# Retention attention and a low-rank channel mixer on one core: when the second weight matrix is loaded, and where the third batch's attention stands

## The chip, the cores and the metric

The program runs on one core of one Trainium2 chip. A core has five engines with instruction queues of their own: TensorE (PE) for matrix products, VectorE (DVE), ScalarE (ACT), GpSimd (POOL), and SyncE (SP), which here only issues transfers. Sixteen DMA engines move data between HBM and the on-chip memory. The time is the device time of one execution in microseconds (us); of several executions the median is given. The span of a profile is the stretch from the first to the last instruction of one profiled execution.

## The reference

Attention without a softmax, with a decay per head, and behind it a mixer over positions of rank 32 and a two-layer channel network:

```python
B, H, S, D = 8, 8, 576, 64
scores = q @ k^T / sqrt(D)
gamma  = 1 - 2.0 ** (-5.0 - arange(H))
ret    = scores * where(i >= j, gamma ** (i - j), 0)
x      = (ret @ v) laid out as (B, S, H * D)          # 8 x 576 x 512
u      = x + (x^T @ U @ V)^T                          # U 576 x 32, V 32 x 576
out    = u + max(u @ w_ch1, 0) @ w_ch2                # w_ch1 512 x 2048, w_ch2 2048 x 512
```

All inputs and the output are float32. The kernel multiplies in bfloat16 and adds up in float32.

## The kernel before

**Tiling.** Batches are taken in pairs. A pair has 1152 positions, which are nine chunks of 128; chunk 4 holds the last 64 positions of the even batch and the first 64 of the odd one. A chunk is named (pair, index), so (1,3) is the fourth chunk of the second pair. Attention is done chunk by chunk with a running state for each head: `SC` makes the scores inside a chunk, `ST` what the chunk adds to the state, `RV` the product of the masked scores with v, `QS` the product of q with the state, `XS` scales the sum into x. The sum of `RV` of one chunk, `SC` of the next, and so on is a "section".

**Getting a chunk ready.** `load` (L225) issues three transfers on SP's queue (six for chunk 4) that bring k, q and v as float32 into 15 staging buffers. `prep` (L562) casts k on DVE (L250) and q on ACT (L252), scales v on POOL (L261), and issues a transposing transfer `qkT<-qk` on SP's queue (L269). `SC` and `QS` read the transposed tile.

**The channel network.** `Y1` (L492) makes one block of 128 hidden features for the positions of a batch: four matrix products into one of three PSUM buffers (`ps_big`), for an odd batch twice, with 4 and with 1 chunk of positions or with 3 and 2; ACT then applies Relu (L505) into `y1`. `Y2` (L529) adds up 16 products over the hidden features for one chunk of positions, four to an item; DVE adds u (L523), and POOL issues the store (L526). w_ch2 comes in eight pieces of two feature blocks each, which `load_w2(f)` (L207) issues on POOL's queue.

**Order.** The program order is written by hand, and every engine and every queue works in that order. `startup` and `first_stretch` (L914) do the first pair's attention and the even batch's first layer. Then the loop at L1047 makes one stage for each b from 1 to 7. In a stage `merge` (L22) runs through the `main` items, which are matrix products of the channel network with a cost in ns each, and puts in between two queues of other items, each with a place between 0 and 1: an item is emitted ahead of the first main item at which the cost done so far has reached its place times the sum of costs. The first queue, `fill`, holds the next batch's attention sections, the casts of the state (on ACT, between the sections), and the mixer (`MA`, `MH`, and `MT`, which from the second pair on is a transposing transfer `uT<-u` on SP's queue). `spread` (L16) gives these items even places from 0 to 0.82. The second queue holds the loads and the preps of later chunks, with the places of the table `places` (L1038).

Stage b=1 has the remaining ten `Y1` blocks of the first odd batch (f=6 to 15; the first six are in `first_stretch`), then `Y2` of both batches of the first pair. Its main items cost 10.8 + 13.8 + 17.3 = 41.9 us. Stages 2, 4 and 6 have 27.6 us of main items, stages 3, 5 and 7 have 34.6 us. Stage 1 holds the attention of the third batch (chunks (1,0) to (1,4)), stage 2 that of the fourth, and so on.

**Weights before.** `first_stretch` issues `load_w2` for 0 and 2 after the last unit of attention, and those for 4 to 14 in a row behind `prep(NI + 1)` (L1017).

Of the kernel before, what the change touches and what calls it, by code (L numbers as in the profile page):

```python
# [10 lines left out]
BF16 = mybir.dt.bfloat16  # L11
# [4 lines left out]
def spread(fill, lead=0.82):  # L16

    n = len(fill)
    return [((k + 0.5) / n * lead, fn) for k, fn in enumerate(fill)]


def merge(main, *queues):  # L22

    total = sum(c for c, _ in main)
    queues = [sorted(q, key=lambda x: x[0]) for q in queues]
    done = 0.0
    for cost, fn in main:
        for q in queues:
            while q and q[0][0] * total <= done:
                q.pop(0)[1]()  # L30
        fn()
        done += cost
    for q in queues:
        for _, fn in q:
            fn()
# [7 lines left out]
def kernel(  # L43
# [11 lines left out]
    nc = tc.nc  # L55
# [5 lines left out]
    P = 128  # L61
    HALF = 64
    NHP = H // 2
    NF = dff // P
# [9 lines left out]
    def pool(name, bufs, **kw):  # L74
        return ctx.enter_context(tc.tile_pool(name=name, bufs=bufs, **kw))

    consts = pool("consts", 1)
# [18 lines left out]

    ident = consts.tile([P, P], BF16, name="ident")
    tri = consts.tile([P, P], BF16, name="tri")
    s_f = consts.tile([P, 2, NHP * D], FP32, name="s_f")
    retz = []  # L100
    triU = consts.tile([P, 2, P], BF16, name="triU")
# [74 lines left out]
    def make_uo():  # L176
        ps = ps_s.tile([P, 5, R], FP32, tag="pss", name="pu_o")
        nc.tensor.matmul(ps, swap, U_E, start=True, stop=True)
        nc.scalar.activation(out=U_O[0:HALF, 1:5, :], in_=ps[0:HALF, 0:4, :], func=AF.Copy)
        nc.scalar.activation(out=U_O[HALF:P, :, :], in_=ps[HALF:P, :, :], func=AF.Copy)  # L180
# [26 lines left out]
    def load_w2(f):  # L207
        nc.gpsimd.dma_start(
            out=w2_sb[:, f:f + 2, :],
            in_=moe_w_ch2[f * P:(f + 2) * P, :].rearrange("(f p) d -> p f d", p=P),  # L210
        )
# [61 lines left out]
    st = {}  # L273
# [454 lines left out]
    def T_J(r, pool_=None, tag="big"):  # L728
        c = ch[0, J]
        pst = (pool_ or ps_big).tile([P, 2 * NHP, P], BF16, tag=tag, name="pst")  # L730
        for j in range(2):
            for hp in range(NHP):
                nc.tensor.transpose(
                    pst[:, j * NHP + hp, r], c["qk"][r, j, hp * P:(hp + 1) * P],
                    ident[r, r])
        if "qkT" not in c:
            c["qkT"] = qkT_pool.tile([P, 2 * NHP, P], BF16, tag="qkT", name="qkT")
        nc.scalar.activation(out=c["qkT"][:, :, r], in_=pst[:, :, r], func=AF.Copy)
# [67 lines left out]
    def startup():  # L806
# [99 lines left out]
        for cc in range(NCC):  # L906
# [4 lines left out]
            else:  # L911
                nc.vector.tensor_copy(out=o, in_=i_)

    def first_stretch():  # L914

        ys = iter([fn for _, fn in y1_items(0)])

        def y(n):
            for _ in range(n):
                fn = next(ys, None)  # L920
                if fn is not None:
                    fn()

        _, MH0, _, outs0 = mixer_items(0, 0, split=True)
        MA1, MH1, MT1, outs1 = mixer_items(0, 1, split=True)
        T_J(HI, ps_s, "pss")
        y(1)
        make_uo()
        SC_J(HI)
        mask_J(HI)  # L930
        y(1)
        acc = pss_tile()
        ST_J(HI, acc)
        Sblk(acc, 0)
        y(1)

        def unit(u, slots, last):
            cast_unit(u)
            load_w1(u)
            scale_u(u, 0, nc.gpsimd)  # L940
            scale_u(u, 1, nc.gpsimd)
            if not last:
                y(1)
            T_u(u, 1, nc.vector)
            T_u(u, 0, nc.scalar)
            y(2)
            SC_u(u, 0, ps_sc, "psc")
            mask_u(u, 0)
            y(1)
            ST_u(u, LO, acc, False)  # L950
            Sblk(acc, slots[1])
            SC_u(u, 1, ps_sc, "psc")
            mask_u(u, 1)
            y(1)
            if not last:
                ST_u(u, HI, acc, False)
                Sblk(acc, slots[2])
            else:
                prep(NI)
                load(*order[NI + 2], (1, 0, 2))  # L960
            RV_u(u, 0)
            QS_u(u, 0, slots[0])
            QS_u(u, 1, slots[1])
            if last:
                RV_J(HI)
                XS_J(HI)
                y(1)
            RV_u(u, 1)
            XS_u(u)

        load(*order[NI], (1, 0, 2))
        load(*order[NI + 1], (1, 0, 2))
        unit(2, (0, 1, 2), False)
        unit(3, (2, 3), True)
        load_w2(0)
        load_w2(2)
        for n in range(2):
            retz.append(ret_pool.tile([P, H, P], BF16, tag="ret", name="ret"))
            nc.gpsimd.memset(retz[n], 0.0)
        xT = [None] * NCC  # L980

        def to_xT(ccs, chunks):
            for cc in ccs:
                if xT[cc] is None:
                    pool_, tag = (ps_sc, "psc") if cc < 2 else (ps_o, "po")
                    t = pool_.tile([P, 2, dm], FP32, tag=tag, name="xT")
                    xT[cc], xT[cc + 1] = t[:, 0, :], t[:, 1, :]
                for i in chunks:
                    nc.tensor.matmul(
                        xT[cc][:, (i - J - 1) * P:(i - J) * P],  # L990
                        st["x", 0][:, i, cc * P:(cc + 1) * P], ident,
                        start=(i == J + 1), stop=True, skip_group_check=True,
                    )

        to_xT((0, 1), (5, 6))
        y(1)
        to_xT((0, 1), (7, 8))
        MA1()
        to_xT((2, 3), (5, 6, 7, 8))
        y(1)  # L1000
        for cc in range(NCC):
            g = slice(cc * R, (cc + 1) * R)
            nc.tensor.matmul(
                xT[cc], st["a", 1][g, :], V4[g, 2 * HALF:2 * HALF + 4 * P],
                start=False, stop=True, skip_group_check=True,
            )
        for cc in range(NCC):
            copy((nc.scalar, nc.vector)[cc // 2], st["uT", 1][:, 1:5, cc, :],
                 xT[cc].rearrange("p (s t) -> p s t", t=P))
        y(16)  # L1010
        Y1, rest = y1_items(1, by_seg=True)
        Y1(0, 0)
        MH1((J,))
        Y1(1, 0)
        prep(NI + 1)
        load(*order[NI + 3], (1, 0, 2))
        for f in range(4, NF, 2):  # L1017
            load_w2(f)
        Y1(2, 0)
        MT1((J,))  # L1020
        MH0(outs0[0])
        for f in range(3, 6):
            Y1(f, 0)
        MH1((5, 6, 7, 8))
        for f in range(6):
            Y1(f, 1)
        return rest[6:]

    with tc.manual_schedule():
        early_consts()  # L1030
        startup()
        y1_left = first_stretch()

        def placed(loads, preps):
            return ([(p, lambda g=g: load(*order[g], (1, 0, 2))) for g, p in loads]
                    + [(p, lambda g=g: prep(g)) for g, p in preps])

        places = {  # L1038
# [6 lines left out]
        }  # L1045
        gl, gp = NI + 4, NI + 2
        for b in range(1, B):  # L1047
            pr, par = divmod(b, 2)
            fill, lead = [], 0.82
            if b + 1 < B:  # L1050
                fill = attn_items((b + 1) // 2, (b + 1) % 2) + mixer_items(
                    (b + 1) // 2, (b + 1) % 2)
            main = y1_items(par) + y2_items(pr, par)
            if b == 1:
                main = y1_left + y2_items(0, 0) + y2_items(0, 1)
                fill = [idle] + fill
            at_l, at_p = places.get(b, ((), ()))
            aux = placed(list(zip(range(gl, gl + len(at_l)), at_l)),
                         list(zip(range(gp, gp + len(at_p)), at_p)))
            gl, gp = gl + len(at_l), gp + len(at_p)  # L1060
            merge(main, spread(fill), aux)
        assert gl == len(order) and gp == len(order)

# [28 lines left out]
```

## Time and profile before

| what | us |
|---|---|
| median of 3 runs | 326.59 (325.59 to 331.24) |
| the profiled execution's own time | 329.42 |
| its span | 327.5 |
| PE busy within the span | 315.9 (96%) |
| DVE busy | 157.3 (48%) |
| ACT busy | 135.5 (41%) |
| POOL busy | 80.2 (24%) |

The granted TensorE clock was 0.999 of full over the span. The page gives the busy time of each engine, the busy share in forty slices, the chain that ended last, and the costliest groups of instructions. Idle time of an engine other than PE costs something only where PE then waits for it. The rows used are shown where the argument uses them; a timeline row has start, duration, engine, line, operation, tile, the number of instructions that were merged, and in brackets the idle time before it with what ended it.

### The profile page before, as it was taken

Reading aid. Unit: us, or ns where it says so; the run is one execution under the profiler, and the core shown is the slowest. Engines: PE = TensorE matmul, PEld = TensorE weight load, DVE = VectorE, ACT = ScalarE, POOL = GpSimd, SP = SyncE. Lnnn points to the kernel's source line nnn. Section 1 sums busy time; section 2 is a strip of 40 time slices with the busy share of each in tenths; the row PEclk is TensorE's granted clock in tenths of the full one; section 3 lists DMA queues with packets and bytes.
Section 4 is the critical chain, followed back from the end, with each engine's and each line's share of the span. In section 5 each row is a group of like instructions: output and inputs, shape, how many; then the busy total and the mean of one; then the engine's idle time right before and its main releaser. Section 6 shows DMA issues by size and latency. Waiting matters only on the chain.

```text
span 327.5 us, 8608 instructions
## 1 busy us (share of the span) xinstructions
PE 315.9 (96%) x3704; PEld 174.4 (53%) x3704; DVE 157.3 (48%) x266; ACT 135.5 (41%) x292; POOL 80.2 (24%) x114
## 2 busy tenths in 40 slices
PE   7799999998899999999999999999999999999996
PEld 3465554654444455457744455457754455467544
DVE  5383554465544456545754357544754465510022
ACT  2557656753110275038720275038720363047400
POOL 5586548012321310122111221122211300110000
PEclk9999999999999999999999999999999999999999
DMA  7999999999996998399992999399993930430012
GB/s 204 233 208 271 228 202 168 197 165 150 253 224 161 256 192 152 90 235 191 178 205 58 246 231 174 90 248 178 204 178 80 211 67 3 115 96 2 0 71 92
DMA packets 151318, 53.27 MB, mean 163 GB/s; under 512 B 131984, under 2 KB 148752, under 8 KB 151280
## 3 DMA queue, kind: packets, MB, share of 16 engines
q1 hardware_dynamic: 144512, 40.40, 69.9%
q0 software_dynamic: 6768, 12.32, 15.9%
q8 instruction: 29, 0.48, 0.6%
q14 instruction: 9, 0.07, 0.1%
HBM read 36.85 MB, written 9.44 MB: 141 GB/s over the span
## 4 chain that ended last, share of the span: by engine, by line
PE 79%; DMA 12%; SPq 5%; POOL 1%; DVE 1%; issue 1%; ACT 0%; DVEq 0%
PE ps_y L534 35%; PE ps_y L500 34%; DMA qkT<-qk 5%; DMA stage_t<-in_q_dram 3%; DMA w_sb<-in_moe_w_ch_dram 3%; SPq L582 2%; PE psc L285 2%; DMA stage_t<-in_v_dram 2%; PE po L340 1%; PE ph L441 1%; PE ps_y L545 1%; PE psc L296 1%; PE po L353 1%; SPq L235 1%; SPq L269 1%; PE pa L414 1%
## 5 line engine op out<-in xcount | busy, mean ns | idle before, releaser
L505 ACT ACTIVATE y<-ps_y 128x384 bf16<-128x384 f32 (+2 forms) x192 | 89.5, 490 | 110.5 <-PE ps_y L500 109.4
L500 PE MATMUL ps_y<-uT,w_sb 128*128 128x512 bf16 (+3 forms) x768 | 132.8, 326 | 1.0 <-DMA w_sb<-in_moe_w_ch_dram 0.5
L534 PE MATMUL ps_y<-w_sb,y 128*128 128x512 bf16 x560 | 126.2, 379 | 0.0
L500 PEld LDWEIGHTS <-w_sb 128*128 128x128 bf16 x768 | 69.8, 98 | 49.9 <-issue 1.3
L534 PEld LDWEIGHTS <-y 128*128 128x128 bf16 x560 | 52.7, 98 | 61.5
L523 DVE TENSOR_TENSOR o_sb<-ps_y,u 128x512 f32<-128x512 f32 (+2 forms) x38 | 25.2, 663 | 76.3 <-PE ps_y L534 74.1
L261 POOL TENSOR_TENSOR vt<-stage_t,vscale 128x512 bf16<-128x512 f32 (+1 forms) x29 | 30.7, 1062 | 77.7 <-DMA stage_t<-in_v_dram 66.0
L526 POOL DMA_DIRECT2D out_dram<-o_sb x31 | 17.2, 554 | 119.4 <-DVE o_sb L523 113.6
L306 DVE TENSOR_TENSOR ret<-psc,tri 64x512 bf16<-64x512 f32 x54 | 36.9, 684 | 0.4
L322 DVE TENSOR_TENSOR s_f<-psc,s_f 128x256 f32<-128x256 f32 x42 | 17.8, 425 | 35.2 <-PE psc L296 33.0
L447 DVE TENSOR_TENSOR u<-ph,xt 128x1024 bf16<-128x1024 f32 (+3 forms) x24 | 21.8, 951 | 11.4 <-PE ph L441 11.4
L252 ACT ACTIVATE qk<-stage_t 128x512 bf16<-128x512 f32 x27 | 16.9, 626 | 16.4 <-DMA stage_t<-in_q_dram 16.4
L364 DVE TENSOR_TENSOR xt<-po,qscale 128x512 bf16<-128x512 f32 x27 | 18.7, 692 | 7.4 <-PE po L353 6.7
L331 ACT ACTIVATE s_sb<-s_f 128x512 bf16<-128x512 f32 (+1 forms) x27 | 15.5, 575 | 1.3 <-DVE s_f L320 1.3
L651 DVE TENSOR_TENSOR ret<-psc,triU 128x1024 bf16<-128x1024 f32 x8 | 9.7, 1223 | 11.4 <-PE psc L643 11.4
L420 ACT ACTIVATE a_sb<-pa 128x128 bf16<-128x128 f32 x8 | 2.2, 278 | 29.4 <-PE pa L414 29.4
L250 DVE CAST qk<-stage_t 128x512 bf16<-128x512 f32 x27 | 12.8, 479 | 0.1
L340 PEld LDWEIGHTS <-ret 128*128 128x128 bf16 x216 | 9.9, 98 | 4.4
L285 PE MATMUL psc<-qkT 64*64 64x64 bf16 x432 | 8.6, 198 | 3.7 <-DMA qkT<-qk 3.7
L600 POOL CAST qk<-stage_t 128x512 bf16<-128x512 f32 x16 | 9.7, 611 | 8.7 <-DMA stage_t<-in_q_dram 6.7
L196 PE MATMUL pw<-ident 128*128 128x512 bf16 x33 | 10.4, 456 | 1.4 <-POOL ident masks.py:199 1.4
L340 PE MATMUL po<-vt,ret 128*128 128x64 bf16 x216 | 10.7, 193 | 0.0
(112 smaller groups left out, 164.8 us busy)
## 6 DMA issues: line engine op xcount, KB each, us to landing
stage_t<-in_k_dram SPq DMA_DIRECT2D x32, 256.0 KB, 5.1
stage_t<-in_q_dram SPq DMA_DIRECT2D x32, 256.0 KB, 5.4
stage_t<-in_v_dram SPq DMA_DIRECT2D x32, 256.0 KB, 5.9
out_dram<-o_sb POOLq DMA_DIRECT2D x31, 256.0 KB, 4.0
w_sb<-in_moe_w_ch_dram POOLq DMA_DIRECT2D x4, 512.0 KB, 8.8
w_sb<-in_moe_w_ch_dram POOLq DMA_DIRECT2D x8, 256.0 KB, 9.9
stage_t<-in_k_dram SPq DMA_DIRECT2D x8, 128.0 KB, 4.9
stage_t<-in_q_dram SPq DMA_DIRECT2D x8, 128.0 KB, 5.0
```

Of the source, the lines that this page charges most:

```text
L252: nc.scalar.activation(out=t[rows, 0, :], in_=c["f", 0][rows].rearrange("p h d -> p (h d)"), func=AF.Copy)
L261: (eng or nc.gpsimd).tensor_tensor(out=c["v"][rows], in0=c["f", 2][rows], in1=vscale[rows, i, :, None].to_broadcast([n, H, D]), op=ALU.mult,)
L306: nc.vector.tensor_tensor(out=ret.rearrange("p (hp hl) i -> p hl hp i", hl=2)[t, :, :, t], in0=c["psc"][t, :, 0:SW].rearrange("p hl (hp i) ...
L322: nc.vector.tensor_tensor(out=f[:, t, :], in0=inc, in1=f[:, 1 - t, :], op=ALU.add)
L340: nc.tensor.matmul(c["po"][:, hl, hp * D:(hp + 1) * D], c["ret"][:, h, :], c["v"][:, h, :], start=(hp == 0), stop=True, skip_group_check=True,
L364: nc.vector.tensor_tensor(out=xt[:, i, :].rearrange("p (hp hl d) -> p hl hp d", hl=2, d=D), in0=c["po"][:, :, 0:NHP * D].rearrange("p hl ( ...
L447: nc.vector.tensor_tensor(out=st["u", par][:, i0 - base:i0 - base + n, w].rearrange("p s (c d) -> p c s d", c=2), in0=ph[k][:, :, 0:n, :], ...
L500: nc.tensor.matmul(ps[:, 0:n, :], w1_sb[:, cc, f * P:(f + 1) * P], st["uT", par][:, c0:c0 + n, cc, :], start=(cc == 0), stop=(cc == NCC - 1),)
L505: nc.scalar.activation(out=st["y1", par][:, f, c0 * P:(c0 + n) * P], in_=ps[:, 0:n, :].rearrange("p s t -> p (s t)"), func=AF.Relu)
L523: nc.vector.tensor_tensor(out=o_sb[:, 0:n], in0=ps[:, 0:n], in1=st["u", par][:, c, w], op=ALU.add)
L526: (nc.sync if last else nc.gpsimd).dma_start(out=out_flat[r0:r0 + P, w], in_=o_sb[:, 0:n])
L534: nc.tensor.matmul(ps, st["y1", par][:, f, c * P:(c + 1) * P], w2_sb[:, f, :], start=(f == 0), stop=(f == NF - 1),)
```

## The change

The change has four parts.

1. A helper `gated_w2(f, block)` copies one element of Relu block `block` of `y1[1]` into a small tile `gate` on POOL, and then issues `load_w2(f)` on POOL's queue. POOL therefore issues the piece once that Relu block is written. `load_w2(0)`, `(2)` and `(4)` stay where they were. Piece 6 stands behind block 3 and piece 8 behind block 4, in the last part of `first_stretch`. Pieces 10, 12 and 14 stand behind blocks 6, 8 and 11 at the places 0.05, 0.11 and 0.17 of stage 1.
2. In stage 1 the fourteen fill items get places of their own: the nine first at 0.20 to 0.60 in steps of 0.05, the others at 0.64, 0.68, 0.72, 0.76 and 0.80. Sections 0 to 5 move from 0.08, 0.19, 0.30, 0.41, 0.52, 0.63 to 0.20, 0.30, 0.40, 0.50, 0.60, 0.68; the mixer's `MH` moves from 0.74 to 0.76.
3. The table `places` of stage 1 is shifted: preps from 0.08, 0.23, 0.34, 0.44, 0.54 to 0.06, 0.20, 0.32, 0.47, 0.60, loads by up to 0.04 either way.
4. In stages 2 to 6 the first prep moves to the start of the stage (0.02 in stage 6), ahead of the first load, and the second prep of stages 2 to 5 moves earlier. In stages 3 and 5 the third prep moves from 0.26 to 0.22 and 0.24. The other loads and preps move later by up to 0.12.

```diff
+    gate = consts.tile([P, 1], BF16, name="gate")
...
+    def gated_w2(f, block):
+
+        nc.gpsimd.tensor_copy(
+            out=gate[0:1, 0:1], in_=st["y1", 1][0:1, block, P:P + 1])
+        load_w2(f)
+
...
         load(*order[NI + 3], (1, 0, 2))
-        for f in range(4, NF, 2):
-            load_w2(f)
+        load_w2(4)
         Y1(2, 0)
         MT1((J,))
         MH0(outs0[0])
         for f in range(3, 6):
             Y1(f, 0)
+            if f > 3:
+                gated_w2(2 * f - 2, f - 1)
...
         places = {
-            1: ((0.13, 0.28, 0.39, 0.49, 0.92), (0.08, 0.23, 0.34, 0.44, 0.54)),
-            2: ((0.0, 0.12, 0.24, 0.92), (0.03, 0.16, 0.30, 0.42)),
-            3: ((0.0, 0.11, 0.23, 0.34, 0.92), (0.03, 0.14, 0.26, 0.37, 0.49)),
-            4: ((0.0, 0.12, 0.24, 0.92), (0.03, 0.17, 0.30, 0.42)),
-            5: ((0.0, 0.11, 0.23, 0.34, 0.92), (0.03, 0.14, 0.26, 0.37, 0.49)),
-            6: ((), (0.06, 0.20)),
+            1: ((0.11, 0.24, 0.41, 0.53, 0.95), (0.06, 0.20, 0.32, 0.47, 0.60)),
+            2: ((0.05, 0.18, 0.30, 0.95), (0.0, 0.09, 0.36, 0.48)),
+            3: ((0.02, 0.15, 0.32, 0.46, 0.95), (0.0, 0.11, 0.22, 0.38, 0.54)),
+            4: ((0.05, 0.20, 0.32, 0.95), (0.0, 0.15, 0.36, 0.48)),
+            5: ((0.03, 0.17, 0.32, 0.46, 0.95), (0.0, 0.13, 0.24, 0.38, 0.54)),
+            6: ((), (0.02, 0.18)),
         }
...
             if b == 1:
                 main = y1_left + y2_items(0, 0) + y2_items(0, 1)
-                fill = [idle] + fill
             at_l, at_p = places.get(b, ((), ()))
+            fill = spread(fill, lead)
+            if b == 1:
+                at = [0.20 + 0.05 * k for k in range(9)] + [0.64, 0.68, 0.72, 0.76, 0.8]
+                fill = [(p, fn) for p, (_, fn) in zip(at, fill)]
+                fill += [(p, lambda f=f, n=n: gated_w2(f, n))
+                         for p, f, n in ((0.05, 10, 6), (0.11, 12, 8), (0.17, 14, 11))]
...
-            merge(main, spread(fill), aux)
+            merge(main, fill, aux)
```

In the table the first tuple of a stage has the places of its loads, the second those of its preps.

## The prediction

> **What bounds the kernel now.** I read the waits of PE first, then the busy times of the stages, then PE's timeline.
>
> ```profile
> PE psc L285 <- DMA qkT<-qk: 3.7, 4, 1.7
> 60.40:110.40 50.00, 47.35 (x516) 24.34 (x515) 23.91 (x40) 13.40 (x33) 9.57 (x13) 1.00 1.11 195
> 110.40:143.70 33.30, 32.92 (x390) 16.11 (x389) 17.99 (x31) 13.32 (x25) 6.34 (x8) 1.00 0.84 170
> 143.70:184.40 40.70, 40.02 (x502) 24.44 (x500) 22.05 (x36) 17.65 (x43) 8.16 (x10) 1.00 1.05 175
> 184.40:217.10 32.70, 32.70 (x390) 16.01 (x389) 18.45 (x31) 13.32 (x25) 6.38 (x8) 1.00 0.99 184
> 217.10:257.10 40.00, 40.00 (x502) 24.45 (x500) 21.43 (x36) 17.65 (x43) 8.31 (x10) 1.00 1.00 178
> 82.40 0.32 PE L285 MATMUL psc<-qkT 64*64 64x64 bf16 x16 [1.73 <-DMA qkT<-qk]
> 88.56 0.32 PE L285 MATMUL psc<-qkT 64*64 64x64 bf16 x16 [0.92 <-DMA qkT<-qk]
> 125.49 0.32 PE L285 MATMUL psc<-qkT 64*64 64x64 bf16 x16 [0.38 <-DMA qkT<-qk]
> 165.01 0.32 PE L285 MATMUL psc<-qkT 64*64 64x64 bf16 x16 [0.68 <-DMA qkT<-qk]
> ```
>
> The window rows are the stages b=1 to 5; behind a stage's length stands PE's busy time, and the last three numbers are the granted clock (1.00 in all), the DMA engines' share and GB/s. PE does not wait in stages 4 and 5, and in the whole program it waits four times for a transposed chunk (first row). These waits are for (1,3) and (1,4) in stage 1 (2.65 us), for (1,8) in stage 2 (0.38), for (2,4) in stage 3 (0.68), together 3.71. The stages of one kind agree with that: stage 2 is 0.6 longer than 4, stage 3 is 0.7 longer than 5. So the change can gain about 3.7 us, 1.1%, and no more: it takes no PE instruction away, and the time ahead of 50 us is left as it is. A loss has no such end. All of the judgement is whether these four waits go, and what comes late in their place.
>
> **Why the transposes are late.** SP and POOL around the weight loads, and how long pieces of w2 took to land (the first two, then the last two):
>
> ```profile
> 50.37 5.41 SPq L235 DMA_DIRECT2D stage_t<-in_v_dram  x1
> 55.94 8.92 SPq L269 DMA_TRANSPOSE qkT<-qk  x1
> 77.37 2.68 SPq L269 DMA_TRANSPOSE qkT<-qk  x1
> 51.83 4.35 POOL L208 DMA_DIRECT2D w_sb<-in_moe_w_ch_dram  x6
> 68.79 1.03 POOL L261 TENSOR_TENSOR vt<-stage_t,vscale 128x512 bf16<-128x512 f32 x1 [12.60 <-DMA stage_t<-in_v_dram]
> L208 POOL DMA_DIRECT2D w_sb<-in_moe_w_ch_dram x2: 721/740/759, 47.6 to 48.3; - x2
> DMA to landing us min/median/max: 6.9/7.3/7.8
> L208 POOL DMA_DIRECT2D w_sb<-in_moe_w_ch_dram x2: 748/750/753, 54.7 to 55.4; - x2
> DMA to landing us min/median/max: 11.9/12.5/13.1
> ```
>
> POOL issues six pieces of w2 from 51.8 to 56.2. Beside them SP needs 5.41 us to issue one load and 8.92 to issue one transpose, so it is at 64.9 before it can issue the load of (1,3); v of (1,2), issued from 50.37, is there at 68.8. Chunk (1,3)'s transpose is issued at 77.37 and ends PE's wait at 82.4 (5.0 us later); (1,4)'s follows on SP's queue behind the three loads of a chunk. The chunks run behind from the flood on.
>
> **Part 1, the gates.** Five copies of one element and five waits on POOL. No row shows such a copy: a one-column memset is the nearest row below, and it costs 0.10, the 64x512 cast above it 0.61. I take 0.10.
>
> ```profile
> 1.25 0.10 POOL L124 MEMSET lnb<- 128x1 f32 x1
> 14.71 0.61 POOL L247 CAST qk<-stage_t 64x512 bf16<-64x512 f32 x1 [0.24 <-DMA stage_t<-in_q_dram]
> 56.82 0.60 ACT L505 ACTIVATE y<-ps_y 128x512 bf16<-128x512 f32 x1 [0.30 <-PE ps_y L500]
> 64.73 0.32 PE L285 MATMUL psc<-qkT 64*64 64x64 bf16 x16
> 100.14 10.47 PE ps_y L534 x48
> 116.11 0.40 PE L340 MATMUL po<-vt,ret 128*128 128x64 bf16 x8
> 116.94 3.63 PE L500 MATMUL ps_y<-uT,w_sb 128*128 128x512 bf16 x16
> ```
>
> A 512-column product takes 10.47/48 = 0.218 us; a Y1 block of stage 1 (four of 512 and four of 128 columns) 1.09; a section 116.94 - 116.11 = 0.83, and section 0, which has no RV, I put at 0.37. Section 0 stood behind four blocks at 64.73, so stage 1 starts at 64.73 - 4.36 = 60.4. Piece 14 is the latest. Its gate waits for Relu block 11: five blocks (5.45), the four large products of the sixth (0.87), a Relu of 0.60, that is 67.3. With the copy POOL issues at 67.4. The piece is needed after ten blocks (10.9), sections 0 and 1 (1.2, now ahead of it) and fourteen products of Y2 (3.05): 60.4 + 15.15 = 75.5. It has 8.1 us to land. The first two pieces of before, each with little of its kind in front, took 6.9 and 7.8; so it is there at 74.3 to 75.2, in time by 0.3 to 1.2. The last pieces of before took 13.1 with five in front: at that end it lands at 80.5 and PE stands 5.0. I take no stall, and keep 0 to 5.0. Piece 12 (gate behind block 8, 64.0) has 3 us more. Behind the gates on POOL stand v of (1,2) and (1,3), used in sections 2 and 3 at 78 us and later, which can wait.
>
> [...]
>
> What it frees: with three pieces instead of eight out by 56 us, the load of v (1,2) and the transpose of (1,1) go ahead of the other five. The load of (1,3) can then be issued some 6 us earlier (8.92 less an issue of 2.68), at about 59. Its casts stand at 0.20 of the stage, 69.4 us, some 10 us behind that.
>
> **Parts 2 and 3, sections and preps of stage 1.** A place becomes a time in the stage by the costs of the main items ahead of it (41.9 us in all) and 0.83 for each section ahead. Section 3, which waited 1.73, moves from 19.8 us of PE work into the stage to 23.3, its prep from 10.95 to 9.0: the time from prep to use grows from 8.9 to 14.2. For (1,4) it grows from 8.6 (16.35 to 24.98) to 12.9 (15.5 to 28.4). The shortfalls were 1.73 and 0.92, and slack added is 5.3 and 4.3, without the 6 us from part 1. Both go. -2.65. What is late next is the mixer's transpose `uT`: MH moves from 36.2 to 37.1 of the stage's 46.9, so it still has 9.8 us where the work behind it (u on DVE, issue, landing) took 102.83 - 99.74 + 4.3 = 7.4 by the rows:
>
> ```profile
> 99.74 0.40 PE L441 MATMUL ph<-a_sb,V 32*128 32x128 bf16 x16
> 102.83 1.32 SPq L458 DMA_TRANSPOSE uT<-u  x1
> uT<-u SPq DMA_TRANSPOSE x9, 4.3
> ```
>
> **Part 4, stages 2 to 6.** A prep at 0 lets the first transpose be issued when DVE's cast is done, about 1.2 us into the stage, instead of behind a load. Stage 2: the prep of (1,8), used in section 3, moves from 6.4 to 3.0 us into the stage; 3.4 earlier, and the wait was 0.38. -0.38. Stage 3 by its rows:
>
> ```profile
> 142.81 2.13 SPq L235 DMA_DIRECT2D stage_t<-in_k_dram  x2
> 145.03 1.50 SPq L235 DMA_DIRECT2D stage_t<-in_q_dram  x2
> 148.20 2.19 SPq L269 DMA_TRANSPOSE qkT<-qk  x1
> 159.77 2.70 SPq L269 DMA_TRANSPOSE qkT<-qk  x1
> DMA to landing us min/median/max: 4.5/5.0/5.8
> 73.55 0.63 ACT L252 ACTIVATE qk<-stage_t 128x512 bf16<-128x512 f32 x1 [1.42 <-DMA stage_t<-in_q_dram]
> 74.09 0.74 ACT L505 ACTIVATE y<-ps_y 128x512 bf16<-128x512 f32 x2
> DMA to landing us min/median/max: 5.4/5.9/6.5
> ACT qk L252 <- DMA stage_t<-in_q_dram: 16.1, 4, 5.2
> L252 ACT ACTIVATE qk<-stage_t 128x512 bf16<-128x512 f32 x27 | 16.9, 626 | 16.4 <-DMA stage_t<-in_q_dram 16.4
> ```
>
> Stage 3 starts at 143.7. Before, SP issued (2,4)'s load first and (2,2)'s transpose behind it at 148.2. Now the transpose goes at 144.9 to 147.1 and the load at 147.1 to 152.5 (it took 148.20 - 142.81 = 5.4). The transposes of (2,3) and (2,4) follow one load each; the latter comes to about 157.6 instead of 159.77, 2.2 earlier, and PE was 0.68 short. -0.68. The price is that (2,4)'s q is issued 4.3 us later while its cast on ACT moves from 11.8 to 9.9 into the stage. ACT works in order: at 73.55 it waited 1.42 for a q, and the next Relu came behind it (row at 74.09). q's second half, issued at about 150.1, lands 5.0 later (median of the loads issued from 142 to 148, the fifth row): 11.4 into the stage, where the cast can start at 10.3. Relus stand meanwhile. PE goes on into three PSUM buffers and first needs the late Relu at 12.46; that Relu ends 0.63 + 0.49 behind the landing, so PE's stall is landing minus 11.35: 0.05 here, 0.85 with 5.8 of landing, nothing with 4.5. I take 0.3 for stage 3, and as much for stage 5, whose order is the same and which had no wait to lose. +0.6. Stages 4 and 6 gain slack only.
>
> **Sum**, against the profiled span: 327.5 - 2.65 - 0.38 - 0.68 + 0.6 = 324.4, 3.1 less, so 326.3 for the profiled execution's own time (329.42). The median of before is 2.8 below that execution; 326.59 - 3.1 = **323.5 us**.
>
> **Rivals.** *Slower: the casts on ACT hold the Relus.* The mechanism is the one of stages 3 and 5. It decides against the change when q of (2,4) and (3,4) lands later than 13.2 into the stage (1.85 us of stall, twice, eats 3.7). With a transpose issue of 2.7 instead of 2.2 and a landing of 6.5 (the longest of the loads issued from 104 to 109, third row from the end) it would be 13.4: two stalls of 2.05, 4.1 in place of the 0.6, and 327.0. ACT's waits speak against: 16.1 of its 16.4 us of waiting for q lie between 60 and 112 us (last two rows), almost none in stages 3 and 5. For it: in these stages the DMA engines are full (shares 1.05 and 1.00). [...]
>
> *The waits come back elsewhere (the change does not do what it says).* The same bytes go through the same full engines in stage 1 (share 1.11), and chunks are late again, one step further on. Then nothing is gained: 326.6, within 1. Against it stands the slack of 4 to 5 us, worked out above.
>
> *The last pieces of w2 come late.* Two to five us at Y2's start, 323.5 + 2 to 5 = 325.5 to 328.5. For it: a margin of only 0.3 to 1.2, with loads of (1,4) beside the piece. Against: one or two pieces out at a time.
>
> **Chances.** Forecast 0.62 (322.3 to 324.6), waits elsewhere 0.10, w2 late 0.15, ACT held 0.09, and 0.04 for a stall that repeats in every stage and that I do not see. The range reaches from all 3.7 gained with half a us of scatter, 322.2, to w2 late at its far end, 328.5. A measurement of this kernel can tell about 2% from no change (6.5 us). Faster by that is beyond the 3.7 that there are: 0.01. Slower by it (over 333.1) takes w2 late and ACT held at once, or the unseen: 0.05. Within: 0.94.
>
> **What would show it.** No wait of PE for `qkT` in stages 1 to 3; the transpose of (1,1) issued in under 4 us; pieces 12 and 14 landed before 75 and no wait of PE L534 for w2; the casts L252 on ACT in stages 3 and 5 with idle time before them that ends with a q's landing, and PE L500 idle behind them by some tenths. Wrong would make it: a landing of piece 14 beyond 8.1 us, q of (2,4) beyond 13 into its stage, or `uT` late at 107.

## The result

The changed kernel takes **324.47 us** (median of 20 runs) against 326.61 for the kernel before beside it: a ratio of **0.9934**, 95% interval 0.9909 to 0.9958. (Ratios are taken over undisturbed runs, so they can differ a little from the quotient of two medians.) The profiled execution took 323.99 with a span of 322.1, against 329.42 and 327.5.

The stages after, by the view of windows (length, then busy time of PE, PEld, DVE, ACT, POOL, clock, DMA share, GB/s), with the part ahead of stage 1 as the first row:

```profile
0.00:59.00 59.00, 54.59 (x785) 30.55 (x786) 32.41 (x56) 34.41 (x69) 34.72 (x57) 1.00 1.13 226
59.00:106.40 47.40, 46.61 (x512) 24.50 (x517) 24.00 (x40) 14.35 (x34) 12.40 (x19) 1.00 1.10 198
106.40:139.00 32.60, 32.44 (x387) 15.97 (x389) 18.08 (x31) 13.19 (x25) 6.33 (x8) 1.00 0.90 175
139.00:179.00 40.00, 39.73 (x499) 24.40 (x501) 21.59 (x36) 17.41 (x43) 7.97 (x10) 1.00 0.91 178
```

Stage 1 takes 47.4 us instead of some 50.1, stage 2 32.6 instead of 33.1, stage 3 40.0 instead of 40.8 (before, counted from PE's first product of each stage, at 110.45 and 143.54): 2.7, 0.5 and 0.8 less, 4.0 in all. PE's waits after 55 us do not name `qkT` any more; the two products that waited for (1,3) and (1,4) now stand without one:

```profile
82.70 0.32 PE L286 MATMUL psc<-qkT 64*64 64x64 bf16 x16
87.87 0.32 PE L286 MATMUL psc<-qkT 64*64 64x64 bf16 x16
```

The other 1.4 of the 5.4 us between the two spans lie ahead of stage 1 (59.0 against 60.4), where the order of instructions is the same up to 50 us. Some 0.6 of it is waits of PE for loads and casts, 0.7 the first ten products (4.45 us before, 3.77 after). This part scatters: in thirteen of the fourteen profiles of this document stage 1 starts between 58.8 and 60.5 us, whatever the edit (section 0 less 1.09 for each block ahead of it).

SP, POOL and ACT after, by their timelines:

```profile
54.27 1.23 SPq L270 DMA_TRANSPOSE qkT<-qk  x1
71.14 2.18 SPq L270 DMA_TRANSPOSE qkT<-qk  x1
66.21 0.18 POOL L917 COPY gate<-y 1x1 bf16<-1x1 bf16 x1 [2.05 <-ACT y L506]
66.66 0.71 POOL L209 DMA_DIRECT2D w_sb<-in_moe_w_ch_dram  x1 [0.27 <-issue]
149.51 0.64 ACT L253 ACTIVATE qk<-stage_t 128x512 bf16<-128x512 f32 x1
```

And from issue to landing, all eight pieces of w2, then the transpose of (1,1), by the instructions of their lines:

```profile
DMA to landing us min/median/max: 4.4/5.4/6.5
DMA to landing us min/median/max: 4.8/4.8/4.8
```

The transpose of (1,1) is issued in 1.23 us instead of 8.92 and lands 4.8 us after its issue; a piece of w2 lands in 4.4 to 6.5 instead of 6.9 to 13.1. That issue scatters too: 1.23 to 4.48 us in the eight profiles with gates, 4.67 to 8.92 in the six without. Piece 14 is issued at 66.66. The row of ACT is the cast of q of (2,4) in stage 3: ACT does not wait for it.

### The profile page after: what moved, and what is told of

Same layout as the page of the kernel before. It is cut to its first block, busy times and chain, and to the rows that moved or that the text cites. A ratio compares the mean times of both kernels' runs of the same rounds, so it can differ in the third digit from the quotient of the medians.

```text
span 322.1 us, 8590 instructions
## 1 busy us (share of the span) xinstructions
PE 312.9 (97%) x3680; PEld 174.0 (54%) x3704; DVE 157.0 (49%) x266; ACT 135.0 (42%) x292; POOL 80.6 (25%) x119
## 4 chain that ended last, share of the span: by engine, by line
PE 91%; SPq 2%; DVE 2%; issue 1%; DMA 1%; ACT 1%; POOL 0%
PE ps_y L501 39%; PE ps_y L535 38%; PE psc L286 2%; PE po L341 2%; SPq L583 1%; DMA stage_t<-in_q_dram 1%; PE ph L442 1%; PE po L354 1%; PE psc L297 1%; PE ps_y L546 1%; PE pa L415 1%; DVE xt L687 1%; PE po L670 1%; PE psc L644 1%; PE pss L708 1%
## 5 line engine op out<-in xcount | busy, mean ns | idle before, releaser
L501 PE MATMUL ps_y<-uT,w_sb 128*128 128x512 bf16 (+3 forms) x768 | 132.7, 326 | 0.5 <-ACT uT L911 0.3
L535 PE MATMUL ps_y<-w_sb,y 128*128 128x512 bf16 x536 | 124.1, 379 | 1.9 <-issue 1.0
L501 PEld LDWEIGHTS <-w_sb 128*128 128x128 bf16 x768 | 69.9, 98 | 49.4 <-issue 1.6
L251 DVE CAST qk<-stage_t 128x512 bf16<-128x512 f32 x27 | 11.6, 434 | 0.1
L197 PE MATMUL pw<-ident 128*128 128x512 bf16 x33 | 9.7, 431 | 1.4 <-POOL ident masks.py:199 1.4
L627 ACT ACTIVATE qkT<-pst 128x1024 bf16<-128x1024 bf16 x5 | 6.3, 1259 | 7.5 <-PE pst L616 7.5
```

Source lines behind the costliest of these rows:

```text
L501: nc.tensor.matmul(ps[:, 0:n, :], w1_sb[:, cc, f * P:(f + 1) * P], st["uT", par][:, c0:c0 + n, cc, :], start=(cc == 0), stop=(cc == NCC - 1),)
L535: nc.tensor.matmul(ps, st["y1", par][:, f, c * P:(c + 1) * P], w2_sb[:, f, :], start=(f == 0), stop=(f == NF - 1),)
```

## The experiments

All kernels were compared with the kernel before on the same chip. Its median was 328.15 us beside the first four, 328.38 beside the second four and 329.10 beside the last four: on these chips it scatters somewhat more (325.1 to 333.9 beside the last four) than beside the main result (325.5 to 331.2).

| kernel | median us | ratio to before, 95% interval |
|---|---|---|
| the kernel before again | 327.89 | 1.0028 (0.9991 to 1.0066) |
| gates only | 327.67 | 0.9990 (0.9952 to 1.0029) |
| stage 1's places only | 326.49 | 0.9924 (0.9884 to 0.9964) |
| places of stages 2 to 6 only | 325.74 | 0.9935 (0.9906 to 0.9963) |
| all but the places of stages 2 to 6 | 325.91 | 0.9914 (0.9879 to 0.9950) |
| all but the gates | 325.40 | 0.9915 (0.9885 to 0.9944) |
| all, piece 14 gated later | 327.69 | 0.9981 (0.9947 to 1.0014) |
| all, q of chunk 4 held | 334.16 | 1.0162 (1.0095 to 1.0228) |
| all, once more | 324.43 | 0.9878 (0.9835 to 0.9922) |
| all but stage 1's places | 326.17 | 0.9923 (0.9889 to 0.9956) |
| all, third piece of w1 earlier | 325.71 | 0.9931 (0.9890 to 0.9971) |
| the same without gates | 326.34 | 0.9922 (0.9881 to 0.9963) |

Most of these intervals overlap, and the parts do not add up: stage 1's places alone and the other places alone each come near the whole change. What one part does is therefore read from PE's waits in the traces; what it is worth in time stays open.

**The kernel before again.** No edit.

> The kernel before once more, unchanged. If the four waits of PE for qkT are the whole cost, they come again in this profile with 3 to 4 us in total, and the time up to stage 1 (section 0 at 64.7 us) repeats within 1.5 us. If the profile shown first was an unlucky one, the waits add up to about 2 us, which is what the medians moved.

PE's waits for a transposed chunk, from its timeline:

```profile
81.62 0.32 PE L285 MATMUL psc<-qkT 64*64 64x64 bf16 x16 [1.34 <-DMA qkT<-qk]
87.50 0.32 PE L285 MATMUL psc<-qkT 64*64 64x64 bf16 x16 [0.64 <-DMA qkT<-qk]
124.55 0.32 PE L285 MATMUL psc<-qkT 64*64 64x64 bf16 x16 [0.51 <-DMA qkT<-qk]
```

Three of the four waits come again, with 2.49 us in total instead of 3.71, and section 0 at 64.20. So the first profile was the higher of the two. 2.5 is near the 2.1 by which the medians differ.

**Gates only.** The places of the kernel before, with the gates:

```diff
+            1: ((0.13, 0.28, 0.39, 0.49, 0.92), (0.08, 0.23, 0.34, 0.44, 0.54)),
+            2: ((0.0, 0.12, 0.24, 0.92), (0.03, 0.16, 0.30, 0.42)),
...
-                at = [0.20 + 0.05 * k for k in range(9)] + [0.64, 0.68, 0.72, 0.76, 0.8]
+                at = [0.82 * (k + 1.5) / 15 for k in range(14)]
```

> Only the gated pieces of w2; sections, preps and loads stay at their old places. Theory (the flood of w2 sets the chunks back by 6 us): the transpose of (1,1) is issued in under 3 us instead of 8.9, and the waits of stage 1 go down from 2.65 us to under 0.4; the waits of stages 2 and 3 stay, so 1.5 to 2.4 us less than before, ratio 0.993 to 0.995. Rival (the same bytes through full DMA engines, only the place of the sections helps): waits of stage 1 above 2 us, ratio 0.998 to 1.000.

PE's waits, then rows of SP's timeline from the transpose of (1,1) on, with DVE's cast of k of (1,2) between them:

```profile
80.08 0.32 PE L286 MATMUL psc<-qkT 64*64 64x64 bf16 x16 [0.88 <-DMA qkT<-qk]
85.71 0.32 PE L286 MATMUL psc<-qkT 64*64 64x64 bf16 x16 [0.39 <-DMA qkT<-qk]
122.59 0.32 PE L286 MATMUL psc<-qkT 64*64 64x64 bf16 x16 [0.34 <-DMA qkT<-qk]
...
54.46 4.42 SPq L270 DMA_TRANSPOSE qkT<-qk  x1
58.97 0.53 SPq L236 DMA_DIRECT2D stage_t<-in_k_dram  x1
...
66.02 0.43 DVE L251 CAST qk<-stage_t 128x512 bf16<-128x512 f32 x1
...
67.02 2.13 SPq L270 DMA_TRANSPOSE qkT<-qk  x1
69.26 1.31 SPq L236 DMA_DIRECT2D stage_t<-in_k_dram  x2
...
73.96 1.73 SPq L270 DMA_TRANSPOSE qkT<-qk  x1
```

1.27 us of waiting stay in stage 1 (1.98 in the profile of before again, 2.65 in the first), and no gain in time can be told. My expectation was wrong: neither under 0.4 us of waiting as the theory had it, nor above 2 as the rival had it, and the issue still took 4.42. SP issues (1,3)'s load at 58.97 and is through at 63.2, but the transpose of (1,2) goes only at 67.02, behind DVE's cast at 66.02, which stands at its old place. Behind it come the six transfers of (1,4), and only then, at 73.96, the transpose of (1,3). So the flood delayed this order, and by this trace the order still holds the chunks back when the flood is gone.

**Stage 1's places only.** w2 in one row, stages 2 to 6 as before:

```diff
-        load_w2(4)
+        for f in range(4, NF, 2):
+            load_w2(f)
...
-            if f > 3:
-                gated_w2(2 * f - 2, f - 1)
...
-                fill += [(p, lambda f=f, n=n: gated_w2(f, n))
-                         for p, f, n in ((0.05, 10, 6), (0.11, 12, 8), (0.17, 14, 11))]
```

> Only stage 1's places for sections, preps and loads; w2 goes out in one row as before, and stages 2 to 6 stay. Theory (each of the two is enough by itself, since 4 to 5 us more from prep to use outweigh waits of 1.73 and 0.92): no wait for qkT in stage 1 although the transpose of (1,1) is still issued in 5 us or more; 1.5 to 2.7 us less than before, ratio 0.992 to 0.995. Rival (only the missing flood helps): waits of stage 1 above 1.5 us, ratio 0.997 to 1.000.

```profile
54.36 6.15 SPq L270 DMA_TRANSPOSE qkT<-qk  x1
121.51 0.32 PE L286 MATMUL psc<-qkT 64*64 64x64 bf16 x16 [0.45 <-DMA qkT<-qk]
```

By SP's timeline the transpose of (1,1) still takes 6.15 us to issue; by PE's there is no wait in stage 1, only one in stage 2. Stage 1's places (sections, preps and loads together) are enough by themselves, as expected. The wait for (2,4) in stage 3 is missing here, too, although its places are the old ones.

**Places of stages 2 to 6 only.** The gates taken out as above, and stage 1 (its row of `places` and the fill's places) as before:

```diff
-            1: ((0.11, 0.24, 0.41, 0.53, 0.95), (0.06, 0.20, 0.32, 0.47, 0.60)),
+            1: ((0.13, 0.28, 0.39, 0.49, 0.92), (0.08, 0.23, 0.34, 0.44, 0.54)),
```

> Only the places of stages 2 to 6. Theory: the waits for (1,8) and (2,4) go (0.38 and 0.68), those of stage 1 stay; 0.5 to 1.1 us less than before, ratio 0.9965 to 0.9985. Rival (ACT's casts of q hold the Relus in stages 3 and 5): idle time of PE in front of ps_y behind the section of (2,2) and of (3,2), and no gain or a loss, ratio 0.999 to 1.004.

```profile
70.69 0.32 PE L286 MATMUL psc<-qkT 64*64 64x64 bf16 x16 [2.15 <-DMA qkT<-qk]
87.30 0.32 PE L286 MATMUL psc<-qkT 64*64 64x64 bf16 x16 [0.61 <-DMA qkT<-qk]
```

By PE's timeline the waits of stages 2 and 3 are gone, and PE does not stand behind a cast. In stage 1 a new one appears: (1,1) was 2.15 late in this execution. In the first profile of before its transpose, issued at 55.94, took 13.8 us to land, at 69.74, and was used at 69.79; here it took 15.1. The median is lower than expected (0.9935, where 1.06 us of waits would be 0.9968); this one profile, which took 327.01, does not show why, and it stays open.

**All but the places of stages 2 to 6.**

```diff
-            2: ((0.05, 0.18, 0.30, 0.95), (0.0, 0.09, 0.36, 0.48)),
+            2: ((0.0, 0.12, 0.24, 0.92), (0.03, 0.16, 0.30, 0.42)),
...
```

> Gates and all of stage 1's places, but stages 2 to 6 as before. Theory (the gain is the sum of the waits that go): no wait for qkT in stage 1, the waits for (1,8) and (2,4), 0.4 to 1.0 us together, stay; 1.3 to 2.5 us less than before, and 0.3 to 1.0 slower than the whole change. Rival (stages 2 to 6 are free of waits anyway once stage 1 runs on time): as fast as the whole change, no wait for qkT at all.

```profile
122.56 0.32 PE L286 MATMUL psc<-qkT 64*64 64x64 bf16 x16 [0.37 <-DMA qkT<-qk]
161.98 0.32 PE L286 MATMUL psc<-qkT 64*64 64x64 bf16 x16 [0.58 <-DMA qkT<-qk]
```

PE's timeline: the waits for (1,8) and (2,4) are there again, 0.95 us against 1.06 in the first profile, and none in stage 1.

**All but the gates.** The gates taken out as in "Stage 1's places only", with all places of the change.

> The whole change but the gates: w2 goes out in one row as before. Theory (the later sections are enough, the gates add nothing to the time): no wait for qkT anywhere, ratio to before as that of the whole change, 0.991 to 0.995. Rival (the flood still costs: a transpose of (1,1) that takes 14 us to land, or the first products of the second layer): a wait of 0.5 us or more in stage 1, ratio 0.996 or above.

PE does not wait for `qkT` anywhere after 55 us, and the ratio, 0.9915, is that of the other variants. With the new places the gates give nothing that can be measured here.

**All but stage 1's places.** Gates, and the places of stages 2 to 6.

```diff
-                at = [0.20 + 0.05 * k for k in range(9)] + [0.64, 0.68, 0.72, 0.76, 0.8]
+                at = [0.82 * (k + 1.5) / 15 for k in range(14)]
...
-            1: ((0.11, 0.24, 0.41, 0.53, 0.95), (0.06, 0.20, 0.32, 0.47, 0.60)),
+            1: ((0.13, 0.28, 0.39, 0.49, 0.92), (0.08, 0.23, 0.34, 0.44, 0.54)),
```

> Gates and the places of stages 2 to 6, with stage 1's sections, preps and loads at their old places. Theory (the sections do the work in stage 1, the gates only halve its waits): waits for (1,3) and (1,4) of 1.0 to 1.5 us stay, none in stages 2 and 3; 0.5 to 1.5 us slower than the whole change. Rival (any two of the three parts are enough): as fast as the whole change.

```profile
79.89 0.32 PE L286 MATMUL psc<-qkT 64*64 64x64 bf16 x16 [0.41 <-DMA qkT<-qk]
86.67 0.32 PE L286 MATMUL psc<-qkT 64*64 64x64 bf16 x16 [1.55 <-DMA qkT<-qk]
```

1.96 us of waiting in stage 1, none behind it, and a median 1.7 above the whole change on the same chip: both a little more than I expected, and the theory's side of it.

**Piece 14 gated later.**

```diff
-                         for p, f, n in ((0.05, 10, 6), (0.11, 12, 8), (0.17, 14, 11))]
+                         for p, f, n in ((0.05, 10, 6), (0.11, 12, 8), (0.26, 14, 15))]
```

> The whole change, but piece 14 is gated by Relu block 15 instead of 11. The piece can be issued 4.4 us later, about 71.3, and lands 4.4 to 6.5 us behind that (w2's landings with the change), 75.7 to 77.8, against a need at 74.1. Theory (a margin of about 2 us is all that the gates leave): PE waits 1.6 to 3.7 us for w2 in the first chunk of the second layer, and the kernel is 1.5 to 3.7 us slower than the whole change. Rival (a lone piece lands in under 3 us): no wait, as fast as the whole change.

POOL's issue of the piece, and PE's first products that need it:

```profile
71.20 0.76 POOL L209 DMA_DIRECT2D w_sb<-in_moe_w_ch_dram  x1 [0.29 <-issue]
76.29 3.18 PE L535 MATMUL ps_y<-w_sb,y 128*128 128x512 bf16 x14 [2.22 <-DMA w_sb<-in_moe_w_ch_dram]
```

The piece takes 5.0 us to land, not under 3 as the rival had it, and PE waits 2.22: the third rival's price, where its condition is met. No gain can be told any more (0.9981).

**The whole change once more.** No edit.

> The whole change once more, on the same chip as the three below. Theory: no wait of PE for qkT behind 55 us, ratio 0.991 to 0.995 as before. Rival (the first profile of it was a lucky one): waits of 0.5 us or more come up in stages 1 to 3.

```profile
74.72 3.18 PE L535 MATMUL ps_y<-w_sb,y 128*128 128x512 bf16 x14 [0.21 <-DMA w_sb<-in_moe_w_ch_dram]
```

No wait for `qkT`, but one of 0.21 for piece 14, which took 7.9 us to land in this execution (6.4 in the first). The gate on block 11 stands with no margin left. The ratio, 0.9878, is below the 0.991 to 0.995 that I expected; it rests on six runs, and its interval reaches to 0.9922.

**q of chunk 4 held.**

```diff
-            3: ((0.02, 0.15, 0.32, 0.46, 0.95), (0.0, 0.11, 0.22, 0.38, 0.54)),
+            3: ((0.115, 0.15, 0.32, 0.46, 0.95), (0.0, 0.11, 0.22, 0.38, 0.54)),
...
-            5: ((0.03, 0.17, 0.32, 0.46, 0.95), (0.0, 0.13, 0.24, 0.38, 0.54)),
+            5: ((0.135, 0.17, 0.32, 0.46, 0.95), (0.0, 0.13, 0.24, 0.38, 0.54)),
```

> The whole change, but in stages 3 and 5 the load of chunk 4 is issued behind the transpose of chunk 3 instead of ahead of it, so q of (2,4) and (3,4) lands about 15 us into the stage, with its cast in ACT's order at 9.9. Theory (ACT stops at the cast, the Relus behind it stop, PE runs out of its three buffers): ACT idle 4 to 5 us in front of the cast, PE idle 2.5 to 4 us in each of the two stages, 5 to 8 us slower than the whole change. Rival (PE has enough buffered work, or takes the section ahead): under 1 us in each, under 2 us slower.

ACT's cast and PE's next products in stage 3, then in stage 5; section 0 of these stages stands at 141.62 and 215.84, so they start at 140.5 and 214.75:

```profile
153.53 0.63 ACT L253 ACTIVATE qk<-stage_t 128x512 bf16<-128x512 f32 x1 [2.41 <-DMA stage_t<-in_q_dram]
154.59 3.86 PE L501 MATMUL ps_y<-uT,w_sb 128*128 128x256 bf16 x28 [1.39 <-ACT y L506]
...
232.35 0.63 ACT L253 ACTIVATE qk<-stage_t 128x512 bf16<-128x512 f32 x1 [7.01 <-DMA stage_t<-in_q_dram]
233.41 5.19 PE L501 MATMUL ps_y<-uT,w_sb 128*128 128x256 bf16 x28 [5.99 <-ACT y L506]
```

The cast starts 13.0 and 17.6 us into the stage. "Landing minus 11.35" gives 1.65 and 6.25; PE waits 1.39 and 5.99. The mechanism of the first rival is as it was priced, though the two stages differ more than the 2.5 to 4 us each that I expected. In time it costs more than the 7.4 us of waiting that it shows (the last section has a part of the rest): 334.16, the median of four runs, is 8.8 over the variant without gates on the same chip and 9.7 over the change's 324.47 on another.

**Third piece of w1 earlier.** In three of the twelve profiles without this edit PE waits 0.54 to 0.99 us near 39.6 for a piece of w1 that POOL issues behind the third unit's casts, and in a fourth 1.07 at 45.74. That is not most of them, as the expectation says, and neither profile of the whole change has the wait.

```diff
+            if not last:
+                load_w1(u)
             cast_unit(u)
-            load_w1(u)
+            if last:
+                load_w1(u)
```

> The whole change, and the third piece of w1 issued on POOL ahead of the casts of the third unit instead of behind them, so about 5 us earlier. In most profiles PE waits 0.5 to 1.1 us for that piece near 39.6 us. Theory: that wait goes and nothing comes in its place, 0.3 to 1.0 us faster than the whole change. Rival (the piece takes the DMA engines from the third unit's k, q and v, whose casts come later): the wait comes up again in front of that unit's transposes, as fast or up to 1 us slower.

```profile
22.24 0.80 POOL L203 DMA_DIRECT2D w_sb<-in_moe_w_ch_dram  x1
30.97 0.51 PE L616 MATMUL pst<-ident,qk 128*128 128x128 bf16 x6 [0.65 <-POOL qk L601]
```

The piece goes out at 22.24 by POOL's timeline instead of 29.11 and PE does not wait for it, but now it waits 0.65 for the third unit's casts. The median is 1.3 above the whole change on the same chip: the rival. The same edit without gates gave 326.34, with 2.23 and 0.39 of that wait in its profile:

> The same earlier piece of w1 without the gates (w2 in one row). Theory (gates add nothing to the time where the sections stand later): as fast as the kernel with gates and the earlier piece, within 0.5 us. Rival: slower by 0.5 us or more, with a wait in stage 1.

Its median is 0.63 above that with gates, but its ratio to before is the lower one (0.9922 against 0.9931): no difference can be told. Its profile has no wait in stage 1. So this pair leaves it open whether the gates are worth some tenths. No variant has a median below that of the change itself, though most intervals overlap with its own.

## Why the prediction was right, and where it was not

The forecast was 323.5 with a range of 322.2 to 328.5; measured were 324.47, within 2% of before and on the side that was forecast.

- **The bound.** The waits are as said: they go with the parts that were meant to remove them, and come back when a part is undone (0.37 and 0.58 without stages 2 to 6; 0.41 and 1.55 without stage 1's places). In the first pair of profiles stages 1 to 3 became 4.0 us shorter for 3.71 of waits. What was mis-sized is this 3.71, the sum that the other terms rest on. It is that of one execution which took 2.8 more than the median; a second profile shows 2.49. Subtracting a difference of one profile from a median gave 3.1 where the medians moved by 2.1. Whether 3.7 is the most that can be gained stays open: beside the last four kernels the ratio was 0.9878, 1.2%, but its interval, 0.9835 to 0.9922, holds 1.1% as well. The lower end of the range was added up 0.2 too low: 326.59 - 3.71 - 0.5 is 322.4.
- **Part 1.** The gates' price was right: nothing to 0.2. The copy takes 0.18, near the lower row, and 0.27 passes between it and the issue. Piece 14 was issued 7.6 us into stage 1 where I had 7.0, and its margin, put at 0.3 to 1.2, was about 1 in one profile and less than nothing (0.21 of waiting) in the other. Its landing, put at 6.9 to 7.8 us, was 6.4 and 7.9. The load of (1,3) was freed as worked out (issued at 58.97 with the gates alone, where I had about 59), but the chunk gained little by it: its transpose went at 73.96 instead of 77.37, since a cast and SP's order held it, and 1.27 us of waits were left.
- **Parts 2 and 3.** -2.65 was right in kind and was done by the places alone: none of the nine profiles with stage 1's new places has a wait for a chunk there, and all five with the old ones have 1.27 to 2.76 us. Later sections and earlier preps were not tried apart. By these traces either could have done it, an estimate: with the new places and w2 still in one row, (1,3)'s transpose was issued 14.4 us into the stage (73.50 - 59.14), and with the 5.2 us to landing that such a transpose took before (median of 27 in the first profile) it would be there at 19.6, ahead of its old use at 20.3; and before it landed 22.0 into it, ahead of its new use at 23.7. `uT` was not late: issued at 99.29, landed 4.3 later, used at 106.31 without a wait.
- **Part 4.** -0.38 and -0.68 went, and are the same two waits that the variant without it shows again. The first stands in all five profiles with the old places of these stages (0.34 to 0.51 us), the second only in two of the five (0.68 and 0.58), and neither in the nine with the new ones. The price of +0.6 for the casts on ACT was wrong: the transpose ahead of (2,4)'s load was issued in 1.29 us and not 2.2, q landed in time, and the cast at 149.51 did not wait; in stage 5 that of (3,4) did not either, and in the second profile of the change it waited 0.23 without holding PE. That term is 0. Its formula was right, to 0.3 us, as the held casts showed. The error and that in the 3.71 pull in opposite directions: without the price the forecast would have been 322.9. That it is only 1.0 off is in part luck.
- **The rivals.** Casts that hold the Relus, and late pieces of w2, are both real. The second is at hand (0.21 us of it in one profile, 2.22 with a gate four blocks later); the first takes a load that is issued 7.3 us into stage 3 instead of 2.7.

## What to carry to other kernels

Where single waits of a us decide, take more than one profile of the kernel before: here the waits for a transposed chunk moved from chunk to chunk and from profile to profile (3.71 us in one profile of before, 2.49 in the other), and the start of stage 1 scattered by 1.7 us in thirteen of the fourteen profiles, where the medians moved by 2.1. Two remedies for one wait did not add up here: new places did what thinning the flood alone did not (no wait in stage 1, where the gates alone left 1.27 us), because a cast and the queue order behind the flood still stood where they were. A cast that waits for a load on ACT, which took its work in order, was priced here by what stood behind it: the landing, less the work that the buffers let PE do (1.65 and 6.25 us by that formula, 1.39 and 5.99 measured).

## What was not expected of the hardware

In the long wait of PE in the held-cast kernel (5.99 us) the granted clock fell from 1.00 to 0.50. Windows of 2 us from 226 us on (the clock is the third number from the end):

```profile
226.00:228.00 2.00, 1.42 (x58) 0.91 (x55) 0.00 (x0) 0.00 (x0) 0.00 (x0) 1.00 0.76 148
228.00:230.00 2.00, 0.00 (x0) 0.00 (x0) 0.00 (x0) 0.00 (x0) 0.00 (x0) 0.83 0.58 127
230.00:232.00 2.00, 0.00 (x0) 0.00 (x0) 1.28 (x4) 0.00 (x0) 0.00 (x0) 0.50 0.82 185
232.00:234.00 2.00, 0.59 (x3) 0.40 (x3) 1.87 (x3) 1.65 (x4) 0.00 (x0) 0.50 0.91 195
234.00:236.00 2.00, 2.00 (x9) 1.10 (x8) 0.00 (x0) 0.66 (x3) 1.04 (x1) 0.50 1.36 222
236.00:238.00 2.00, 2.00 (x16) 1.36 (x15) 0.00 (x0) 1.77 (x5) 0.37 (x1) 0.96 1.27 212
```

PE stands from 227.4 to 233.4. With one step from 1.00 to 0.50 and one back, an estimate from these rows, the 0.83 of the second row puts the fall at about 229.3, some 2 us into the wait, and the 0.96 of the last its end at about 236.2. So the first 2.8 us of work after the wait run at a clock of 0.50, which costs some 1.4 us by the same estimate; the 28 products at 233.41 took 5.19 us, the 28 of the same form at 154.59 took 3.86. Behind the waits of 2.22 us (piece 14), 2.15 us (places of stages 2 to 6 only) and 1.39 us (the held casts in stage 3) the products took no longer than elsewhere: 3.18 us for fourteen, as behind the 0.21 of the whole change once more; 2.35 for sixteen of L501, as with the gates only; 3.86 for 28, as in the whole change once more at 224.74 without a wait. The mean clock of the first two executions was 1.0, that of the held casts 0.988. But in the profile of the earlier piece of w1 without gates a wait of 2.23 us was enough; PE stands there from 31.4:

```profile
33.60 0.40 PE L616 MATMUL pst<-ident,qk 128*128 128x128 bf16 x2 [2.23 <-POOL qk L601]
32.00:34.00 2.00, 0.40 (x2) 0.13 (x2) 0.10 (x1) 0.00 (x0) 0.90 (x2) 0.90 0.78 215
34.00:36.00 2.00, 1.61 (x9) 1.07 (x10) 0.00 (x0) 0.75 (x1) 1.71 (x3) 0.50 1.04 303
36.00:38.00 2.00, 2.00 (x19) 0.69 (x21) 0.00 (x0) 1.23 (x3) 1.80 (x3) 0.75 1.06 287
```

By the same working the clock is 0.50 from about 33.6 to 37.0, over some 3 us of work, a loss of 1.5 us, an estimate in the same way; the mean clock of this execution was 0.994. So a wait of 6 us cost about 1.4 us more than its length, and one of 2.2 us cost as much more in one profile and nothing that shows in two others; what decides that is not shown here.
